# A list scheduler for the second layer of a sigmoid-attention and two-layer kernel, and fixed projection banks in the first layer

## Chip, cores and metric

One core of one Trainium2 chip. The metric is the device time of one execution in microseconds (us); the runs of the kernel before took 1118.6 us in the median of three (1116.41 to 1119.95).

## The reference

Sigmoid attention on 4 batches of 12 heads, sequence 448, head size 64, gives x of 1792 tokens by 768. Two layers follow:

```python
scores = scale * q @ k.T - log(S);  x = (sigmoid(scores) @ v)      # attention, heads side by side
h = x @ w_in                        # 768 -> 2048
x = (h - tanh(h)) @ w_out           # first layer, 2048 -> 768
gate = sigmoid(x @ w_gate)          # 768 -> 1536
x = (gate * (x @ w_val)) @ w_out2   # second layer, 1536 -> 768
```

All inputs of the layers are fp32 values handed over as 64-bit words whose bits the kernel decodes itself.

## The kernel before

**Split numbers.** Each operand of a matmul is split in a high part (ACT copy into fp32r) and a low part (a subtraction on DVE or POOL); a product is three matmuls: high by high, high by low, low by high (`mm3`, L363). A matmul has 128 rows and 448 columns. In tile names, `g`/`gg` are activations (index 0 high, 1 low), `w`, `w_b`, `w_t` weights, `po`/`pq` projections, `ph` hidden sums, `pa pb pc pe` the four PSUM banks of the second layer, `acc` the sums of a layer's output.

**First layer.** 32 steps (N1 = 32): 8 groups of 256 hidden columns, 4 batches each. Step i runs on TensorE the 36 matmuls `ph` of step i+1 (`hidden_mm`) and then the 36 matmuls `po` of step i, six groups of six, one for each 128 output rows (`project_group`, L456). The activation of step i+1 (`hidden_act`, L385) is a chain of ACT instructions (`th sq cut q1 q2`, then the high part) and DVE instructions (`a b c d e`, then the low part `f`). Groups 0, 2 and 4 are added into `acc` by DVE (L471). Groups 1, 3 and 5 are, from step 4 on, seeded: ACT copies the running sum into the bank first (`seed`, L451), the matmuls add to it, and ACT copies it back (L522). All six come out of a pool of four banks, `pb`, in which a new tile takes a bank that was given back; `step` (L501) writes the order of the instructions out by hand, with lists `extra` of things to slip in between groups. LASTSEED = 29 is the first step without seeds.

A weight of the first layer is decoded once (`decode`, L138: one ACT instruction, then four on DVE, L148 to L163). In most first-layer steps one unit of the second layer's weights is decoded as well (`keeping`, tile `mk`) and written to DRAM (`kept`); 21 of 36 units are done so, and the other 15 late, in the second layer, through a tile `mq`, staged in two SBUF buffers.

**Second layer.** 12 blocks (two passes of six; a pass holds two batches). A block has a gate half of seven products (a11, s1, s2, a12, s3, s4, a22: a Strassen-like form over 2 x 2 blocks of activations and weights, `TERMS`, L557), a value half of the same seven, and the twelve projection groups of the block before as fillers between the products of the gate half. A product is nine matmuls, a projection group six. Bank contents move on between products: after a11 ACT copies pa to pb (L720), after s2 pb to pc (L724); s3 adds to pc, and DVE reads the sum (L731 in the gate half, L759 in the value half) before a22 adds to pc again. The value half ends with the high part of `gg` on ACT (L737) and its low part on POOL (L740).

For each block three weight units are loaded from DRAM (`load_m`, L608) and split (`split_pieces`, L616): DVE differences (L639 to L644), ACT highs (L175), POOL lows (L178). When they are issued is decided by `background` (L658): after each product or group it advances a counter by 1.8 or 1.2 us, issues at most one split piece whose load should have come, then loads, then at most one late decode step. `require` (L678) issues whatever a product still needs. The operands of a pass (`operand`, L578) are sums on DVE (L576), highs on ACT (L590) and lows on DVE or POOL (L592); those of pass 0 are placed by hand in steps 29 and 30 and in block 0, those of pass 1 by `turn` (L795) as the value half of block 5 gives places back.

**From the first to the second layer.** The loop at L893 runs steps 0 to 30. After it the first layer's tiles are closed, the PSUM pools are replaced by one with `pa pb pc pe` and four projection banks (L940), the loads and splits are queued, and the projection of step 31 (`groups1`, L484) runs as the fillers of block 0.

Of the kernel before, what the change touches and what calls it, by code (L numbers as in the profile page):

```python
# [32 lines left out]
def kernel(  # L33
# [161 lines left out]

    def keeping(j):
        box = []

        def piece(s):
            def run():  # L200
                if s == 0:
                    if late[0]:
                        if not mq:
                            mq.append(stp.tile([128, 2 * WC], I32, tag="st0", name="mq"))
                        m = mq[0][:, j % 2 * WC:][:, :WC]
                    else:
                        m = wp.tile([128, WC], I32, tag="wh0", name=f"mk{j}")
                    box.append(m)
                    box.extend(decode(NU1 + j, m))
                box[1 + s]()  # L210
                if s == 3:
                    n, h = divmod(j, 2)
                    if h == 0:
                        kept[n] = keep_p.tile([128, 2 * WC], I32, tag=f"kept{n}", name=f"kept{n}")
                    nc.sync.dma_start(out=kept[n][:, h * WC:(h + 1) * WC], in_=box[0])
                    whole.add(j)
# [4 lines left out]
    late = [False]  # L221
    mq = []
# [162 lines left out]
    def hidden_act(i):  # L385
# [45 lines left out]
        def e():  # L431
            nc.vector.copy_predicated(y, mk.bitcast(I32), h)
            nc.scalar.activation(out=gt[:, 0], in_=y, func=AF.Copy)
# [6 lines left out]
        return [sq, th, cut, q1, q2], [a, b, c, d, e, f]  # L440
# [4 lines left out]
    def pb_tile(name):  # L445
        if len(pb_pool) == 1:
            return pb_pool[0].tile([128, 512], F32, tag="pb", name=name)
        n = pb_n[0] = (pb_n[0] + 1) % 4
        return pb_pool[1].tile([128, 512], F32, tag=f"pb{n}", name=name)

    def seed(name, at, d):  # L451
        po = pb_tile(name)
# [3 lines left out]
    def project_group(name, at, gt, outs, d, first, dst=None, po=None, evict=True):  # L456

        seeded = po is not None
        if not seeded:
            po = pb_tile(name)  # L460
# [5 lines left out]
        if not evict:  # L466
            return po
# [16 lines left out]
    def groups1(i):  # L484

        at, gt, outs = outs1(i)
        for d in range(KD):
            def run(d=d):
                project_group(f"po{i}_{d}", at, gt, outs, d, False)
# [4 lines left out]
    LASTSEED = N1 - 3  # L494
# [539 lines left out]
```

## Time and profile before

| | us |
|---|---|
| median of the runs | 1118.6 |
| profiled execution, its own time | 1120.31 |
| span of that execution, first to last instruction | 1118.5 |
| TensorE busy | 1091.0 |
| VectorE (DVE) busy | 816.3 |
| ScalarE (ACT) busy | 613.2 |
| GpSimd (POOL) busy | 407.9 |

Shares are of the span. Matmuls are pipelined, so two that follow each other overlap in the busy time; what TensorE loses is better read from how far apart runs of matmuls start. `x36` after a row is the number of instructions merged in it, and `[0.28 <-ACT acc L522]` says how long the engine was idle before the row and which instruction ended that.

### The profile page before, as it was taken

What the parts mean: (1) busy time and instruction counts of PE and PEld (TensorE: products, weight loads), DVE (VectorE), ACT (ScalarE), POOL (GpSimd) and SP (SyncE); (2) the same over time, 40 slices, a digit from 0 to 9 for tenths busy, and PEclk for the clock granted to TensorE, in tenths of its full rate; (3) what the DMA queues carried; (4) which work ended last, traced back from release to release, by engine and by line L of the source; (5) the groups of instructions that cost most, each with busy time, mean ns of one, the idle gap of its engine ahead of it and who ended that gap; (6) DMA issues with size and microseconds to landing.
All of it is one profiled execution on the core that took longest, in us unless ns stands there. A gap on an engine that the chain in (4) does not pass through costs nothing.

```text
span 1118.5 us, 15946 instructions
## 1 busy us (share of the span) xinstructions
PE 1091.0 (98%) x6085; PEld 967.8 (87%) x6085; DVE 816.3 (73%) x1115; ACT 613.2 (55%) x855; POOL 407.9 (36%) x411
## 2 busy tenths in 40 slices
PE   9999989999999999999999999999998999999998
PEld 5677779998888888899888888988997999999997
DVE  4778657898898989899868979978468555454444
ACT  6778745676767767777656544434336334334320
POOL 5455300011111111011115367566466656446530
PEclk9999999999999999999999999999999999999999
DMA  7666302334242424234300256563111411112102
GB/s 199 189 187 191 115 1 85 99 104 134 81 135 99 142 99 141 87 124 131 112 29 29 98 177 205 166 200 129 57 57 57 156 58 57 58 56 72 70 1 99
DMA packets 40205, 119.79 MB, mean 107 GB/s; under 512 B 6081, under 2 KB 21441, under 8 KB 40129
## 3 DMA queue, kind: packets, MB, share of 16 engines
q1 hardware_dynamic: 36896, 116.38, 32.1%
q0 software_dynamic: 3072, 2.17, 0.9%
q8 instruction: 48, 0.79, 0.3%
q10 hardware_dynamic: 160, 0.23, 0.1%
q14 instruction: 29, 0.23, 0.1%
HBM read 99.09 MB, written 19.66 MB: 106 GB/s over the span
## 4 chain that ended last, share of the span: by engine, by line
PE 87%; DVE 5%; ACT 3%; POOL 2%; issue 1%; DMA 1%; SPq 0%; ACTq 0%; DVEq 0%
PE ph L365 21%; PE po L365 20%; PE pq L365 14%; PE pb L365 6%; PE pa L365 6%; PE pc L365 6%; PE pv L349 5%; PE sa L314 4%; PE pe L365 3%; PE sl L326 1%; POOL a L592 1%; PE pv L342 1%; POOL gg L740 1%; DVE mq L157 0%; DMA st<-in_w_in_dram 0%
## 5 line engine op out<-in xcount | busy, mean ns | idle before, releaser
L365 PE MATMUL po<-g,w 128*128 128x448 f32 x1152 | 246.0, 367 | 3.8 <-DVE acc L471 2.0
L365 PEld LDWEIGHTS po<-g,w 128*128 128x128 f32 x1152 | 210.3, 188 | 33.7 <-ACT acc L522 7.8
L365 PE MATMUL ph<-x,w 128*128 128x448 f32 x1152 | 235.8, 362 | 0.2 <-ACT at L318 0.2
L365 PEld LDWEIGHTS ph<-x,w 128*128 128x128 f32 x1152 | 215.8, 187 | 15.3 <-ACT at L318 0.6
L178 POOL TENSOR_TENSOR w<-m,w 128x384 fp32r<-128x384 f32 x64 | 63.7, 1018 | 389.0 <-ACT w L175 311.8
L365 PE MATMUL pq<-gg,w 128*128 128x448 f32 x864 | 183.8, 363 | 5.0 <-POOL gg L740 2.4
L365 PEld LDWEIGHTS pq<-gg,w 128*128 128x128 f32 x864 | 161.4, 187 | 18.6 <-POOL gg L740 3.1
L178 POOL TENSOR_TENSOR w_t<-mm,w_t 128x384 fp32r<-128x384 f32 x92 | 100.9, 1126 | 129.8 <-ACT w_t L175 54.2
L471 DVE TENSOR_TENSOR acco<-pq,acco 128x448 f32<-128x448 f32 x120 | 72.2, 619 | 33.4 <-PE pq L365 32.9
L365 PE MATMUL pa<-a,w_b 128*128 128x448 f32 x432 | 94.2, 362 | 0.0
L365 PEld LDWEIGHTS pa<-a,w_b 128*128 128x128 f32 x432 | 81.1, 188 | 5.5
L402 ACT ACTIVATE y<-ph 128x896 f32<-128x896 f32 x32 | 29.4, 920 | 78.4 <-PE ph L365 78.4
L471 DVE TENSOR_TENSOR acc<-po,acc 128x448 f32<-128x448 f32 x93 | 57.1, 618 | 20.3 <-PE po L365 20.3
L318 ACT ACTIVATE at<-sa,bias_s 128x896 f32<-128x896 f32 x72 | 67.3, 1008 | 7.9 <-PE sa L314 7.8
L175 ACT ACTIVATE w_b<-mm 128x768 fp32r<-128x768 f32 (+1 forms) x48 | 32.5, 679 | 63.1 <-PE pb L365 30.5
L740 POOL TENSOR_TENSOR gg<-sg,gg 128x448 fp32r<-128x448 f32 x44 | 62.0, 1439 | 13.0 <-ACT gg L737 12.8
L175 ACT ACTIVATE w_t<-mm 128x768 fp32r<-128x768 f32 x48 | 39.9, 842 | 47.9 <-DVE mm L644 34.2
L178 POOL TENSOR_TENSOR w<-mm,w 128x384 fp32r<-128x384 f32 x44 | 48.5, 1124 | 45.5 <-ACT w L175 43.3
L178 POOL TENSOR_TENSOR w_b<-mm,w_b 128x384 fp32r<-128x384 f32 x46 | 51.0, 1130 | 32.7 <-ACT w_b L175 21.7
L349 PE MATMUL pv<-at,vt 128*64 128x224 f32 x576 | 61.3, 363 | 0.0
L145 ACT ACTIVATE m<-st 128x768 f32<-128x768 f32 x32 | 28.9, 903 | 56.7 <-POOL w L178 55.1
L349 PEld LDWEIGHTS pv<-at,vt 128*64 128x64 f32 x576 | 40.1, 140 | 19.7 <-issue 8.0
(102 smaller groups left out, 1861.0 us busy)
## 6 DMA issues: line engine op xcount, KB each, us to landing
mm<-kept SPq DMA_DIRECT2D x36, 768.0 KB, 4.3
st<-in_w_out_dram SPq DMA_DIRECT2D x28, 768.0 KB, 4.5
st<-in_w_in_dram SPq DMA_DIRECT2D x16, 768.0 KB, 4.3
st<-in_w_gate_dram SPq DMA_DIRECT2D x12, 768.0 KB, 5.0
st<-in_w_val_dram SPq DMA_DIRECT2D x12, 768.0 KB, 5.0
kept<-mk SPq DMA_DIRECT2D x21, 384.0 KB, 5.6
kept<-mq SPq DMA_DIRECT2D x15, 384.0 KB, 5.6
kt<-in_k_dram SPq DMA_DIRECT2D x48, 112.0 KB, 4.1
```

Source lines behind the costliest of these rows:

```text
L145: nc.scalar.activation(out=mf, in_=hi.bitcast(F32), func=AF.Abs)
L175: nc.scalar.activation(out=w0, in_=mf, func=AF.Copy)
L178: (low or nc.gpsimd).tensor_tensor(out=w1[:, r], in0=mf[:, r], in1=w0[:, r].bitcast(F32), op=ALU.subtract)
L314: nc.tensor.matmul(pa[:, j, :S], kk[r, ki, c], qq[r, qi], start=(i == 0), stop=(i == 2),)
L318: nc.scalar.activation(out=at[:, :, c], in_=pa[:, :, :S], func=AF.Sigmoid, bias=bias_s, scale=qk_scale,)
L326: nc.tensor.matmul(pl[h * KL:(h + 1) * KL, j, :SH], kt[r, KR:], qt[r, h * SH:(h + 1) * SH], start=True, stop=True,)
L342: nc.tensor.matmul(po[j * D:(j + 1) * D, h, :SH], vt[r, j, NCH - 1], al[r, j], start=True, stop=False,)
L349: nc.tensor.matmul(po[j * D:(j + 1) * D, h, :SH], vt[:, j, c], at[:, j, c, h * SH:(h + 1) * SH], start=False, stop=(c == NCH - 2),)
L365: nc.tensor.matmul(o, w(i), xv(j), start=first and n == 0, stop=last and n == 2, skip_group_check=seeded,)
L402: nc.scalar.activation(out=y, in_=h, func=AF.Tanh)
L471: nc.vector.tensor_tensor(out=at[:, d], in0=po[:, :S], in1=at[:, d], op=ALU.add)
L740: low.tensor_tensor(out=gt[t][:, 1, j], in0=sg[t][:, j], in1=gt[t][:, 0, j].bitcast(F32), op=ALU.subtract,)
```

## The change

1. *First layer, steps 4 to 27.* The four projection banks get fixed places by a table over the parity of the step and the group, and the seed of group 5 is emitted right after the copy-out of group 1, no longer after group 2. In `project_group` all matmuls that read the high part of the activation come first. In product the same: the low operand part is read last.
2. *Steps 28 to 30* run in a new function `tail_step`: step 28 has no seeds (TAIL2 = 28), steps 29 and 30 have seeds of groups 1, 3 and 5, each emitted after the group before it. The activation chain becomes a task.
3. *A list scheduler.* `Task` holds instructions with an engine (v DVE, a ACT, g POOL, s the DMA queue), a planned cost, what they follow and a gate; the tasks are ordered by due time. After each group or product `spend` advances a clock by 1.2 or 1.8 us and issues every task instruction that by the planned costs ends within that slot plus a limit (0.9 us for DVE, 1.0 for ACT; less after some products), or on POOL and the DMA queue starts within it. `must` issues an instruction at once. Weight units, operands, late decodes and the low parts of gg are tasks.
4. *Block 0* has all six groups of step 31 after s2 (SHARE0); its tiles sg and p5 lie in the buffer x7, which before was the second staging buffer of late decodes; that buffer is used for staging again from block 1. The tiles of the first layer are closed, and the second weight unit's buffer opened, when the chain of step 31 has been issued (`settle`).
5. *Block 5* has the fillers in the value half (SHARE_END).
6. Step 27 gets a kept decode, so 22 units are decoded in the first layer and 14 late.

The core of the diff:

```diff
+    SLOT = (
+        {1: 0, 0: 1, 3: 2, 2: 3, 5: 0, 4: 1},
+        {1: 2, 0: 3, 3: 0, 2: 1, 5: 2, 4: 3},
+    )
...
-        for j, (_, w) in enumerate(outs):
-            mm3(
-                po[:, :S], lambda a: w[:, a, d], lambda a: gt[:, a, j],
-                j == 0 and not seeded, j == len(outs) - 1, seeded,
-            )
+        for a, c in ((0, 0), (1, 0), (0, 1)):
+            for j, (_, w) in enumerate(outs):
+                nc.tensor.matmul(
+                    po[:, :S], w[:, a, d], gt[:, c, j],
+                    start=n == 0 and not seeded, stop=n == last, skip_group_check=seeded,
+                )
...
         post(1)
+        pre(5)
         c()
         q2()
         group(2)
-        pre(5)
...
+    def tail_step(i, act, dve):
...
+        def group(d):
+            p = None
+            if d % 2 and i > TAIL2:
+                p = seeds.pop(d)
+            p = project_group(f"po{i}_{d}", at, gt, outs, d, False, p, evict=False)
+            if d % 2 == 0 and i > TAIL2:
+                seeds[d + 1] = must("a", 0.55, lambda: None) and seed(f"po{i}_{d + 1}", at, d + 1)
+            spend(1.2)
...
+        chain = Task(f"c{i}", now[0] + (9.0 if i < N1 - 2 else 3.0))
...
+        def start(self):
+            kinds, f, after, gate = self.ops[self.at]
+            t = 0.0 if gate is None else gate()
+            if t is None:
+                return None
+            t = max([t, now[0]] + [self.end[i] for i in after])
+            ways = [(max(t, busy[e]) + cost, max(t, busy[e]), e) for e, cost in kinds.items()]
+            if len(ways) > 1 and not self.haste and ways[1][0] < self.due - SPARE:
+                return ways[1]
+            return min(ways)
...
+    def spend(length, ease=0.9, ease_a=1.0):
+        if last_chain and last_chain[0].at == len(last_chain[0].ops):
+            settle()
+        end = now[0] + length
...
+                if (t if e in "gs" else done) > end + (dict(v=ease, a=ease_a).get(e, 0.0)):
+                    continue
+                task.go(at)
...
+            kinds = dict(v=0.6, g=1.3) if FLEX or n in (0, 1, 2, 18) else dict(g=1.3)
+            task.add(kinds, low(slice(0, HC), False), [h])
+            return task.add(kinds, low(slice(HC, None), True), [h])
...
+            t = task.add(dict(v=1.2), ta, [b1, b22])
+            t = task.add(dict(v=0.7), lambda: tb(0), [t])
+            t = task.add(dict(v=0.7), lambda: tb(1), [t])
...
+        t = task.add(dict(a=0.95), a, (), gate)
+        t = task.add(dict(v=1.4), lambda: box[2](), [t])
+        t = task.add(dict(v=1.2), lambda: box[3](), [t])
+        task.add(dict(v=1.2), c2, [t])
...
+            spend(1.8, 0.2 if term == "s3" else 0.9, 0.4 if term in ("a11", "s2") else 0.8)
...
+        def finish(t, ready):
+            task = g_task[k, t] = Task(f"g{k}_{t}", now[0] + (6.0 if t == 0 else 8.0))
...
+                task.add(dict(v=0.7, g=1.4) if FLEX or k == NK - 1 else dict(g=1.4), f, [h])
...
+    SHARE0 = dict(s2=12)
+    SHARE = dict(s2=2, a12=4, s3=7, s4=10, a22=12)
+    SHARE_END = dict(a11=2, s1=4, s2=6, a12=8, s3=10, s4=12)
```

SPARE is 2.0 us, FLEX and SEED are False.

## Rows read from the trace of the kernel before

**Rows 1.** The page, busy time of the engines over the span.
```profile
PE 1091.0 (98%) x6085; PEld 967.8 (87%) x6085; DVE 816.3 (73%) x1115; ACT 613.2 (55%) x855; POOL 407.9 (36%) x411
```

**Rows 2.** The chain of waits, in order of time: start us, us.
```profile
217.68 7.56 PE po L365 x36
...
557.31 7.57 PE po L365 x36
564.87 7.21 PE ph L365 x36
...
655.91 2.40 PE pq L365 x12
...
906.09 2.40 PE pq L365 x12
...
1064.49 2.40 PE pq L365 x12
```

**Rows 3.** Waits from 214 to 565 us: total us, times, longest us.
```profile
PEld po L365 <- ACT acc L522: 6.8, 24, 0.3
PEld po L365 <- ACT po L453: 6.3, 24, 0.3
```

**Rows 4.** Timeline of one step, 453 to 461 us (start us, us).
```profile
453.59 4.80 PEld L365 LDWEIGHTS po<-g,w 128*128 128x128 f32 x24
...
458.10 0.52 ACT L522 ACTIVATE acc<-po 128x448 f32<-128x448 f32 x1
...
458.67 1.11 PEld L365 LDWEIGHTS po<-g,w 128*128 128x128 f32 x6 [0.28 <-ACT acc L522]
...
459.45 0.53 ACT L453 ACTIVATE po<-acc 128x448 f32<-128x448 f32 x1
...
460.04 1.11 PEld L365 LDWEIGHTS po<-g,w 128*128 128x128 f32 x6 [0.26 <-ACT po L453]
```

**Rows 5.** Timeline of TensorE from step 30 into block 0.
```profile
610.01 1.48 PE L365 MATMUL po<-g,w 128*128 128x448 f32 x6 [2.04 <-DVE acc L471]
...
619.56 1.28 PE L365 MATMUL po<-g,w 128*128 128x448 f32 x5 [1.14 <-DVE g L436]
...
646.90 3.59 PE L365 MATMUL pc<-a,w_t 128*128 128x448 f32 x9 [2.07 <-DVE pe L759]
```

**Rows 6.** Waits of TensorE over the span; then its timeline near the end.
```profile
PE pc L365 <- DVE pe L759: 4.9, 3, 2.1
PE pb L365 <- ACT pb L720: 3.2, 4, 1.1
...
PE pq L365 <- POOL gg L740: 2.4, 2, 1.8
...
1099.25 0.47 PE L365 MATMUL pq<-gg,w 128*128 128x448 f32 x1 [0.56 <-ACT gg L737]
1099.91 14.48 PE L365 MATMUL pq<-gg,w 128*128 128x448 f32 x71 [0.19 <-DVE gg L740]
```

**Rows 7.** Windows: length, busy us (count) of PE PEld DVE ACT POOL, clock, DMA.
```profile
480.00:510.00 30.00, 30.00 (x148) 26.99 (x147) 28.06 (x35) 21.70 (x32) 3.99 (x4) 1.00 0.40 132
648.00:651.00 3.00, 3.00 (x12) 2.67 (x11) 2.97 (x5) 0.83 (x1) 0.12 (x1) 0.64 0.58 205
690.00:730.00 40.00, 39.79 (x198) 36.63 (x197) 35.75 (x45) 18.33 (x28) 26.33 (x22) 1.00 0.57 186
890.00:930.00 40.00, 40.00 (x202) 37.49 (x201) 19.30 (x28) 14.94 (x23) 21.78 (x21) 1.00 0.18 62
```

**Rows 8.** Single lines: count, shortest, median, longest ns, first and last start us.
```profile
L157 DVE SCALAR_TENSOR_TENSOR mk<-st,mk x21: 957/959/960, 171.8 to 543.0; 128x768 int32<-128x768 int32 x21
L157 DVE SCALAR_TENSOR_TENSOR mq<-st,mq x15: 952/1515/1914, 635.5 to 772.9; 128x768 int32<-128x768 int32 x15
L639 DVE TENSOR_TENSOR mm<-mm x24: 944/950/1917, 580.8 to 1062.3; 128x768 f32<-128x768 f32 x24
L740 POOL TENSOR_TENSOR gg<-sg,gg x44: 1132/1470/1877, 651.2 to 1063.3; 128x448 fp32r<-128x448 f32 x44
```

More of the change, by code (lines that the diff above doesn't have):

```diff
@@ L194, with parked @@
     early = []
+    def parked(j, m):
+        n, h = divmod(j, 2)
+        if n not in kept:
+            kept[n] = keep_p.tile([128, 2 * WC], I32, tag=f"kept{n}", name=f"kept{n}")
+        nc.sync.dma_start(out=kept[n][:, h * WC:(h + 1) * WC], in_=m)
+        whole.add(j)
     def keeping(j):
@@ L211, in run @@
                 if s == 3:
[L212 to L216, printed above, removed]
+                    parked(j, box[0])
             return run
         return [piece(s) for s in range(4)]
-    late = [False]
-    mq = []
     whole = set()
@@ new lines, in prepare, with known, gate, one @@
+        done_at = {}
+        def known(*names):
+            def gate():
+                got = [done_at.get(n, free(n[4:]) if n[:4] == "free" else None) for n in names]
+                return None if None in got else max(got)
+            return gate
+        BEFORE = dict(
+            s1=("freesums1",), s2=("freesums2", "sums1", "a11"), s4=("freesums4", "sums2", "s1"),
+            s3=("freesums3", "sums4", "s2"),
+        )
+        def one(term, due):
+            task = op_task[ps, term] = Task(f"x{term}_{ps}", due)
+            after = []
+            task.haste = term in BEFORE
+            if term in BEFORE:
+                def add(c):
+                    def f(eng):
+                        sums(term, ps, c, eng)
+                        task.haste = c < KH - 1
+                        if c == KH - 1:
+                            done_at["sum" + term] = task.end[-1]
+                    return f
+                for c in range(KH):
+                    after = [task.add(dict(v=0.7, g=1.4), add(c), (), known(*BEFORE[term]))]
+            def high():
+                xo[ps, term] = x_tile(PLACE[ps][term], f"{term}_{ps}")
+                nc.scalar.activation(out=xo[ps, term][:, 0], in_=src[term], func=AF.Copy)
+            h = task.add(dict(a=1.35), high, after, known("free" + term))
+            for c in range(KH):
+                def low(eng, c=c):
+                    t = xo[ps, term]
+                    eng.tensor_tensor(
+                        out=t[:, 1, c], in0=src[term][:, c], in1=t[:, 0, c].bitcast(F32),
+                        op=ALU.subtract,
+                    )
+                    if c == KH - 1:
+                        done_at[term] = max(task.end)
+                task.add(dict(v=0.7, g=1.4), low, [h])
@@ L596 @@
+        for i, term in enumerate(TERMS):
+            one(term, due + 1.8 * i)
     m_t = {}
     wk = {}
-    done = {"slot": 0}
-    FETCH = 6.5
-    loads = []
-    splits = []
     order = [0, 1]
@@ L688, with require_x @@
+    BASE = dict(s2=("s1", "a11"), s4=("s2", "s1"), s3=("s4", "s2"))
+    def require_x(ps, term):
+        if ps:
+            for j in sorted(de_task):
+                de_task[j].finish()
+        for other in BASE.get(term, ()):
+            require_x(ps, other)
+        op_task[ps, term].finish()
     PRODUCT = {
@@ L946 @@
-        pb_pool.append(pm[0])
-        late[0] = True
-        late_u.append(NU1 + NPRE - len(early) // 4)
-        fetch(late_u[0] + 1)
-        preps += [
-            lambda: operand(0, "s3", nc.vector), lambda: operand(0, "s4", nc.vector),
-            lambda: operand(0, "a22", nc.vector),
-        ]
-        free_at[0] = 16.0
-        for n in order[1:]:
-            loads.append(n)
-            splits += split_pieces(n)
+            if i >= TAIL2:
+                chain = tail_step(i, act, dve)
+                for term in {TAIL2: ("a11", "a12"), TAIL2 + 1: LATER}.get(i, ()):
+                    x_free[0, term] = now[0] + 0.5
+                continue
```

564 lines of the change are left out of this document (383 added, 181 removed).

## The prediction

> **What bounds the kernel now.** I read the page's engine line first: TensorE is counted busy for 98% of the span [rows 1]. Overlapping matmuls count as busy, so this says only that TensorE is the bound; what it loses has to be read from the pace. The chain of waits gives the pace: 12 matmuls of 448 columns take 2.40 us and a ph run of 36 takes 7.21, 0.200 us each [rows 2]. From step 4 to step 27 each po run of 36 takes 7.56 or 7.57 us instead. The excess over 0.200 us per matmul, stage by stage, all from [rows 2]:
>
> - Steps 4 to 27: from 217.68 to 557.31 lie 23 steps, 339.63 us against 23 x 14.40 = 331.20, and the 24th loses 0.37 more: **8.8 us**.
> - Transition, 564.87 to 655.91: ph of steps 29 to 31 (108 matmuls), po of 28 to 31 (144), block 0 (126) and three products of block 1 (27) are 405 matmuls, 81.0 us; it takes 91.04: **10.0 us**.
> - Blocks 1 to 6, 655.91 to 906.09: six blocks of 198 matmuls are 237.6 us; it takes 250.18: **12.6 us**.
> - Blocks 7 to 11: 906.09 to 1064.49 is 158.40, exactly 4 x 39.6: **nothing**.
> - The end: TensorE idles 0.56 us, and the next matmuls start 0.66 instead of 0.20 us later [rows 6]: **1.0 us**.
>
> Together 32.4 us. No order of this work can save more than that after 217 us, as nothing of the arithmetic goes.
>
> The waits name what ends the loss. In the steps it is ACT twice, 24 times each [rows 3]. In one step [rows 4] group 4's weight load starts at 458.67, right after ACT's copy-out at 458.10 (L522, the eviction of group 1), so group 4 sits in group 1's bank; group 5's load starts at 460.04, after the seed of group 5 at 459.45 (L453), which ACT runs behind q2. In the transition TensorE waits 2.04 us for a DVE sum, 1.14 us for the low half of g31, then 2.07 us for a DVE read of pc [rows 5]. After that last wait nine matmuls take 3.59 us, where nine take 1.8; the clock granted in 648 to 651 is 0.64 of full, so part of that stretch ran at 1.2 GHz [rows 7]. In the second layer the waits are for a DVE read of pc or pe (4.9 us), for ACT's copy into pb (3.2 us), and for POOL's low halves gg (2.4 us) [rows 6]. DVE is loaded where they lie: 35.75 of 40 us in 690 to 730, where late decodes run, 19.30 in 890 to 930, where none do [rows 7].
>
> **Part by part.** *Fixed banks and an earlier seed (steps 4 to 27).* With the table, group 4 takes group 0's bank, evicted by DVE long before, and group 5 takes group 1's. The seed of group 5 is emitted straight after the copy-out of group 1 and ahead of q2. In the step shown ACT ends that copy at 458.62; the seed takes 0.53 and ends near 459.15. The loads of groups 0 to 3 begin at 453.59 [rows 4], so group 5's is due five groups of 1.2 us later, at 459.59. So both waits go. q2 comes 0.5 us later; behind it on ACT stand the copy of a weight and the copy-out of group 3, and DVE's L427 waits for it, by up to 0.5 us; DVE's idle time covers that in a step without a kept decode. In steps with a kept decode DVE is busy 28.06 of 30 us [rows 7], 13.8 us of a 14.77 us step, under the new 14.40. If that cover were gone the step would stay at 14.77. Bounds 0 to 8.8 lost; I take 0.3 left, since the margin on the seed is 0.4 us.
>
> *High halves first.* Same number of matmuls and loads; a low half is now read 0.8 us into a projection group and 1.2 us into a product. It costs nothing, and takes up to 0.8 us off waits like the 1.14 us on g31 and the 0.19 us at the end.
>
> *Steps 28 to 31 and block 0.* Step 28 loses its seeds: six DVE sums instead of three, 1.9 us more on DVE, in a step with no decode. The kept decodes become 22 and the late ones 14; one decode moves from DVE's loaded stretch into step 27, with its fetch and its write to DRAM on SP's queue, long before block 3 reads it. Steps 29 and 30 get three seeds each. Such a seed is put on ACT right after the group before it, behind whatever background work the scheduler has already issued there, up to 1.0 us past the end of the slot by its own costs. A group lasts 1.2 us, so each of the six can be late by 0 to 0.9 us (1.0, a copy-out and a seed of 0.55, less 1.2): 0 to 5.4, and I take 1.0, as ACT's real costs (0.53 for a copy against 0.55 planned) run ahead of the plan. The activation chain of step 31 no longer stands behind operand work by position: it has the earliest due time. Its twelve instructions of about 1 us need some 10 us, and 7.2 + 3 x 1.8 = 12.6 us pass between ph31 and po31. I take 1.0 (0 to 3.2, the first two waits of [rows 5]). The second weight unit is loaded only when that chain has ended, 3 to 6 us into block 0; by the planned costs load 5.0, first split 2.1, differences 2.6 and second split 2.1 make 11.8, and the value half starts 19.8 us into the block: 1.5, bounds 0 to 5. Together **3.5 left of 10.0**, with bounds 0 to 13.6, so a loss is possible here.
>
> *Blocks 1 to 6.* Background work on DVE may run at most 0.2 us past the product s3, and on ACT 0.4 us past a11 and s2. The DVE join then ends 0.85 us after s3, and a22, which overwrites what it reads, comes 1.8 us after it; the pb and pc copies have the same 1.8 us. These are the waits of [rows 6]. The late decodes get one staging buffer in block 0 instead of two, and their due times spread them further: 14 decodes of about 3 us on DVE. In block 5 the projections of block 4 go into the value half, so the operands of pass 1 get 27 instead of 12.6 us to replace those of pass 0. Behind each join on DVE stand only sums into four rotating banks, 3.6 us of slack. I take **2.0 left of 12.6**; bounds 0 to 12.6.
>
> *What speaks against it* is the two-input work on DVE. A decode's L157 takes 957 to 960 ns in the first layer, where POOL is nearly idle, and 1515 ns in the median, 1914 at most, in block 0 to 3 [rows 8]; L639 goes from 950 to 1917. The planner costs these at 1.2 always. The extra 0.97 us of an L639 ahead of a join puts its end at 1.82 us, still at the edge, so by the rows I add nothing to the 2.0. The Trainium skill (SBUF — State Buffer, Who interferes with whom) says that a DVE instruction with two SBUF inputs and a POOL instruction that reads SBUF exclude each other, the second waiting for the whole of the first; the doubled rows agree. By that rule a join behind one 1877 ns POOL instruction [rows 8] would end at 2.7 us and cost 0.9; on all 12 gate and value joins of six blocks that is 11, and the time about 1104.
>
> *The end*: 0.8 of 1.0 left, since the joins and the high half still follow s4. Blocks 7 to 11 have nothing to win.
>
> **Sum.** Left are 0.3 + 3.5 + 2.0 + 0.8 = 6.6 of 32.4, a gain of 25.8. The profiled execution took 1120.3 (span 1118.5 and 1.8 around it), so 1094.5; the median of the runs, 1118.6, stands 1.7 under it: **1092.8, say 1093**.
>
> **Rivals.**
> 1. *DVE stays late where POOL works.* The planner advances its clock by 1.8 and 1.2 us whatever happens and knows no interference, so DVE runs behind its plan in the transition and in the blocks with decodes. For: the stretched rows [rows 8] and 35.75 of 40 us [rows 7]. Against: decodes are spread, and lows of operands and first weights can go to either engine. The transition keeps its 10.0 and blocks 1 to 6 half of 12.6: gain 8.5 + 6.3 + 0.2 = 15.0, **1104**. (The Trainium skill's rule, in SBUF — State Buffer, would bring it about; by its count above the time is the same.)
> 2. *The first layer keeps its pace*, because DVE at 13.8 of 14.4 us takes over as soon as ACT's two waits go. For: 0.6 us a step is little room. Against: each fourth step to step 20 has no kept decode and lets DVE catch up. The 8.5 go: **1101**.
> 3. *The order barely changes*: the scheduler puts second-layer work about where the hand-written counters put it, and the change is its banks alone. For: blocks 7 to 11 were at 39.6 by hand. Against: the s3 and a11 limits target waits that are there. Gain 9.5: **1109**.
> 4. *Slower: POOL's low halves gg come late.* In most blocks the lows of weights and of gg may run on POOL alone. gg of half 0 is read 1.8 + 5.4 + 0.8 = 8.0 us after s4 ends; two joins and the high half by plan (2.3) and two lows at 1470 ns [rows 8] need 5.2, so 2.8 us of margin. If the scheduler issues five or more weight lows ahead, 1.0 to 1.5 us each, all 36 matmuls of a half stand behind the wait in TensorE's queue. At 3.0 us in 11 blocks that is 33: **1126**; from 2.3 us a block on, the gain is gone. Against: POOL is busy 21.78 of 40 us [rows 7], gg has a due time 6 or 8 us ahead, and POOL work is issued only when it can start within the slot; today it cost 2.4 us in all.
>
> **How the numbers follow.** Forecast 0.62, rivals 1 to 4: 0.17, 0.10, 0.06, 0.05. A measurement here tells 0.3%, 3.4 us, from no change. All but rival 4 are faster by more; part of a bad transition together with rival 3 could land within it: 0.02. The forecast's own range is 1088 (1.5 us left) to 1099. Rivals 1 and 2 are taken in, 3 and 4 left out: 1087 to 1105.
>
> **What would show it.** Right: po runs of 7.20 in steps 4 to 27, no ACT releaser there; ph29 to the first pq in under 86 us; no wait for pe L759 or pb; blocks 1 to 6 at 39.6 to 40.2; no stretch with a lower clock in block 0. Wrong: 7.5 us po runs (rival 2); pc waiting for DVE behind an instruction of 1.5 us or more (rival 1); equal stalls at the same products (rival 3); pq waiting for POOL in block after block (rival 4).

## The result and the profile after

The changed kernel took 1104.97 us in the median of four runs (1104.83 to 1105.82), the kernel before 1117.71 beside it (1116.41 to 1119.95): a ratio of 0.9882, with the 95% interval from 0.9866 to 0.9897. A second set of runs gave 1103.62 against 1118.48, 0.9876 (0.9859 to 0.9892). So it is faster by 1.2%, some 13 us, about half of the 25.8 forecast, and the time lies inside the range only just, at its upper edge of 1105.

The profiled execution took 1104.88, with a span of 1103.1: 15.4 us under the 1118.5 of before. The profiled execution of before (1120.31) was 2.6 us slower than the median of the runs beside after, so stages read from the two profiles add up to more than the 13 us of the medians. The losses below are worked out as in the prediction, as what TensorE's matmuls start later than 0.200 us after one another.

| stage | before | forecast left | after |
|---|---|---|---|
| steps 4 to 27 | 8.8 | 0.3 | 0.3 |
| transition, ph of step 29 to the first pq | 10.0 | 3.5 | 7.8 |
| blocks 1 to 6 | 12.6 | 2.0 | 8.6 |
| blocks 7 to 11 | 0 | 0 | 0 |
| end | 1.3 | 0.8 | 1.7 |
| sum | 32.7 | 6.6 | 18.4 |

On TensorE's timeline of after ph of step 29 starts at 555.47, the first pq at 644.24 and that of block 7 at 890.44, so the transition takes 88.77 against 81.0 and blocks 1 to 6 take 246.2 against 237.6. The end of before is 1.3 by the same measure, not the 1.0 of the prediction: the first pq starts 0.73 us late, not 0.56, and the next 0.46, with 0.11 behind it. The sums differ by 14.3; another 0.8 us had gone before step 4 (the first row of the chain below stands at 216.91, that of [rows 2] at 217.68), which differs by more than that between executions of one kernel (po of step 4 starts at 216.75 in this profile of after and at 215.41 in a second one), and the last 0.3 lies behind the last matmul.

The page of after, its busy time (as [rows 1]) and the granted clock in 40 slices of the span:

```profile
PE 1084.3 (98%) x6085; PEld 974.2 (88%) x6085; DVE 809.3 (73%) x1112; ACT 617.7 (56%) x861; POOL 427.4 (39%) x432
...
PEclk9999999999999999999999899999999999999999
```

The busy shares tell as little as before. The one 8 in the clock's line is the slice from 607 to 634 us, which comes back below.

The chain of waits of after, in order of time (start us, us), as [rows 2]:

```profile
216.91 7.21 PE po L468 x36
...
548.42 7.21 PE po L468 x36
555.63 7.20 PE ph L361 x36
...
890.60 2.40 PE pq L468 x12
...
1049.00 2.40 PE pq L468 x12
```

The po runs of 7.56 are now 7.21. From 890.60 to 1049.00 lie 158.40 us, four blocks at 39.6, as before.

The waits of after from 214 to 565 us (total, times, longest), as [rows 3]:

```profile
...
ACT y L398 <- PE ph L361: 40.3, 24, 3.2
DVE acc L481 <- PE po L468: 11.5, 6, 3.7
...
```

ACT and DVE wait for TensorE, as they did before. No row of PE or PEld is left in this view; both ACT releasers of [rows 3] are gone. The timeline of one step shows why (as [rows 4]):

```profile
447.16 7.20 PEld L468 LDWEIGHTS po<-g,w 128*128 128x128 f32 x36
...
451.67 0.52 ACT L536 ACTIVATE acc<-po 128x448 f32<-128x448 f32 x1
...
452.22 0.55 ACT L456 ACTIVATE po<-acc 128x448 f32<-128x448 f32 x1
...
452.70 1.03 ACT L407 ACTIVATE s<-mk,gb 128x896 f32<-128x896 f32 x1
```

All 36 loads are one unbroken row. The seed of group 5 ends at 452.77; the load of that group is due at 447.16 + 5 x 1.2 = 453.16. The margin is the 0.4 us that the prediction had worked out.

**Where the rest stayed.** The waits of TensorE in after, over the span (total, times, longest), as the first part of [rows 6]:

```profile
PE pq L468 <- POOL gg L1064: 3.5, 3, 1.8
...
PE pb L999 <- ACT pb L1012: 1.8, 1, 1.8
PE po L468 <- ACT g L431: 1.6, 1, 1.6
...
PE pq L468 <- DVE w L853: 1.1, 1, 1.1
PE pb L999 <- DVE s L768: 0.8, 1, 0.8
```

The wait for the DVE read of pc or pe is gone, and of four pb waits one is left. What is left lies in two places. The first is block 0. The timeline of after there (start us, us; in brackets the idle time and what ended it):

```profile
594.82 0.55 ACT L585 ACTIVATE acc<-po 128x448 f32<-128x448 f32 x1 [1.81 <-PE po L468]
...
595.73 0.91 ACT L395 ACTIVATE u<-ph 128x896 f32<-128x896 f32 x1
...
602.01 1.10 DVE L423 SCALAR_TENSOR_TENSOR ph<-s,ph 128x896 f32<-128x896 f32 x1
...
603.81 2.65 DVE L768 TENSOR_TENSOR s<-acc,s 128x448 fp32r<-128x448 f32 x3 [0.70 <-ACT s L762]
...
606.38 1.17 DVE L428 COPY_PREDICATED y<-mk,ph 128x896 f32<-128x896 int32 x1
606.51 0.47 PE L999 MATMUL pb<-s,w_t 128*128 128x448 f32 x1 [0.80 <-DVE s L768]
...
608.58 10.61 PE L468 MATMUL po<-g,w 128*128 128x448 f32 x36 [1.60 <-ACT g L431]
...
610.58 8.24 PEld L468 LDWEIGHTS po<-g,w 128*128 128x128 f32 x32 [0.76 <-DVE g L434]
```

The activation chain of step 31 begins at 592.10 (y, L398) and its high half ends just before 608.58. Its second ACT instruction stands in ACT's queue behind a copy-out (594.82) for which TensorE had not yet finished the group, so ACT does nothing for 1.81 us; and its last DVE instruction before the high half (606.38) stands behind three low parts of an operand, some 3.3 us after the chain's DVE instruction before it (602.01) ended. TensorE waits 0.80, does one matmul, waits 1.60, and then needs 10.61 us for 36 matmuls that take 7.36 elsewhere.

The second place is the boundary between the passes, the end of block 5 and the start of block 6:

```profile
841.42 1.33 ACT L762 ACTIVATE s<-acc 128x1344 fp32r<-128x1344 f32 x1 [0.23 <-DVE acc L629]
...
842.65 0.83 ACT L842 ACTIVATE w<-mm 128x768 fp32r<-128x768 f32 x1
842.82 1.63 POOL L768 TENSOR_TENSOR s<-acc,s 128x448 fp32r<-128x448 f32 x1 [1.98 <-ACT s L762]
842.85 4.79 DVE L768 TENSOR_TENSOR s<-acc,s 128x448 fp32r<-128x448 f32 x4
843.38 0.53 ACT L1012 ACTIVATE pb<-pa 128x448 f32<-128x448 f32 x1
...
843.96 2.08 PE L999 MATMUL pb<-s,w_t 128*128 128x448 f32 x9 [1.78 <-ACT pb L1012]
...
847.12 5.94 POOL L1064 TENSOR_TENSOR gg<-sg,gg 128x448 fp32r<-128x448 f32 x4
...
848.68 0.47 PE L468 MATMUL pq<-gg,w 128*128 128x448 f32 x1 [1.85 <-POOL gg L1064]
...
850.15 2.88 PE L468 MATMUL pq<-gg,w 128*128 128x448 f32 x7 [0.99 <-POOL gg L1064]
```

ACT's copy into pb stands behind the high part of an operand, which itself waited for a DVE sum, and behind the high part of a weight. Then the low halves of gg on POOL come late.

Windows of after (length, busy us and count of PE PEld DVE ACT POOL, clock, DMA), and below them one of before, as [rows 7]. Block 6 starts 19.1 us later in before than in after, and so does this window, to hold the like work as 797 to 850 of after:

```profile
609.00:615.00 6.00, 5.86 (x16) 4.71 (x16) 5.33 (x6) 3.59 (x4) 3.82 (x4) 0.52 0.40 131
690.00:730.00 40.00, 40.00 (x201) 37.49 (x201) 36.26 (x47) 17.51 (x28) 28.35 (x21) 1.00 0.59 195
797.00:850.00 53.00, 48.53 (x239) 44.30 (x238) 43.86 (x51) 27.20 (x36) 43.92 (x35) 1.00 0.17 56
848.00:853.00 5.00, 3.33 (x9) 2.74 (x10) 4.59 (x4) 0.00 (x0) 5.00 (x4) 0.73 0.46 157
```

```profile
816.10:869.10 53.00, 48.13 (x235) 43.42 (x234) 40.68 (x47) 25.57 (x34) 35.85 (x27) 1.00 0.13 46
```

In 609 to 615 the granted clock is 0.52, so TensorE ran at 1.2 GHz nearly throughout. The 36 matmuls took 10.61 - 7.36 = 3.25 us more than elsewhere. Not all of that is the clock: the restart and the wait of a weight load for the low half of g31 (0.76 us on PEld) are in it. In experiment 5 the same 36 took 7.80 us behind a like wait at full clock, so the clock cost some 2.8 us. In 690 to 730, where the late decodes run, DVE is fuller than before (36.26 against 35.75 us) and TensorE loses nothing. Towards the boundary POOL is busy 43.92 of 53 us where it had 35.85 at the like place, and DVE 43.86 where it had 40.68.

**At the end** the planner gave two of the last four low halves of gg to POOL. The timeline of after:

```profile
1083.77 1.07 PE L468 MATMUL pq<-gg,w 128*128 128x448 f32 x4 [0.56 <-ACT gg L1059]
1083.86 3.04 POOL L1064 TENSOR_TENSOR gg<-sg,gg 128x448 fp32r<-128x448 f32 x2 [12.27 <-ACT gg L1059]
...
1085.45 13.88 PE L468 MATMUL pq<-gg,w 128*128 128x448 f32 x68 [0.61 <-POOL gg L1064]
```

POOL needs 3.04 us for two; TensorE waits 0.61 us, where in [rows 6] it waited 0.19 for DVE.

### The profile page after: what moved, and what is told of

Its sections match the earlier page's. It is cut to its first block, busy times and chain, and to the rows that moved or that the text cites. A ratio compares the mean times of both kernels' runs of the same rounds, so it can differ in the third digit from the quotient of the medians.

```text
span 1103.1 us, 15973 instructions
## 1 busy us (share of the span) xinstructions
PE 1084.3 (98%) x6085; PEld 974.2 (88%) x6085; DVE 809.3 (73%) x1112; ACT 617.7 (56%) x861; POOL 427.4 (39%) x432
## 4 chain that ended last, share of the span: by engine, by line
PE 93%; DVE 3%; ACT 2%; POOL 1%; issue 1%; DMA 0%; SPq 0%; ACTq 0%; POOLq 0%
PE ph L361 21%; PE po L468 21%; PE pq L468 15%; PE pa L999 8%; PE pc L999 7%; PE pb L999 7%; PE pv L345 5%; PE sa L310 4%; PE pe L999 3%; PE sl L322 1%; PE pv L338 1%; DMA st<-in_w_in_dram 0%; PE pz L1173 0%; ACT at L314 0%; POOL gg L1064 0%
## 5 line engine op out<-in xcount | busy, mean ns | idle before, releaser
L468 PE MATMUL po<-g,w 128*128 128x448 f32 x1152 | 240.0, 366 | 2.1 <-ACT g L431 1.6
L468 PEld LDWEIGHTS po<-g,w 128*128 128x128 f32 x1152 | 216.0, 189 | 21.0 <-ACT g L431 1.9
L468 PE MATMUL pq<-gg,w 128*128 128x448 f32 x864 | 184.4, 364 | 5.1 <-POOL gg L1064 3.5
L468 PEld LDWEIGHTS pq<-gg,w 128*128 128x128 f32 x864 | 162.5, 188 | 17.8 <-POOL gg L1064 4.5
L853 POOL TENSOR_TENSOR w_t<-mm,w_t 128x384 fp32r<-128x384 f32 x90 | 96.8, 1105 | 137.9 <-ACT w_t L842 137.5
L853 POOL TENSOR_TENSOR w_b<-mm,w_b 128x384 fp32r<-128x384 f32 x54 | 59.8, 1128 | 15.0 <-ACT w_b L842 13.3
L1064 POOL TENSOR_TENSOR gg<-sg,gg 128x448 fp32r<-128x448 f32 x42 | 55.1, 1341 | 24.4 <-ACT gg L1059 24.4
L398 ACT ACTIVATE y<-ph 128x896 f32<-128x896 f32 x32 | 29.4, 919 | 59.2 <-PE ph L361 59.0
L853 POOL TENSOR_TENSOR w<-mm,w 128x384 fp32r<-128x384 f32 x44 | 47.1, 1094 | 21.3 <-ACT w L842 20.7
L310 PE MATMUL sa<-sp 64*128 64x448 f32 x432 | 51.1, 376 | 0.2 <-ACT at L314 0.2
```

The lines of the kernel that those rows point to most:

```text
L310: nc.tensor.matmul(pa[:, j, :S], kk[r, ki, c], qq[r, qi], start=(i == 0), stop=(i == 2),)
L398: nc.scalar.activation(out=y, in_=h, func=AF.Tanh)
L468: nc.tensor.matmul(po[:, :S], w[:, a, d], gt[:, c, j], start=n == 0 and not seeded, stop=n == last, skip_group_check=seeded,)
L853: eng.tensor_tensor(out=w1[:, r], in0=quarters(lo, hi)[:, r], in1=w0[:, r].bitcast(F32), op=ALU.subtract,)
L1064: eng.tensor_tensor(out=gt[t][:, 1, j], in0=sg[t][:, j], in1=gt[t][:, 0, j].bitcast(F32), op=ALU.subtract,)
```

## The experiments

Eleven further kernels ran, and the kernel after once more. Edits are against the kernel after, except in the first and in the hand-ordered one. A kernel with one execution is named so. A loss is the sum of TensorE's excess over 0.200 us per matmul in the stage.

**1. The banks and the seed alone**, put into the kernel before:

```diff
+    SLOT = (
+        {1: 0, 0: 1, 3: 2, 2: 3, 5: 0, 4: 1},
+        {1: 2, 0: 3, 3: 0, 2: 1, 5: 2, 4: 3},
+    )
...
+        pre(5)
         c()
         q2()
         group(2)
-        pre(5)
```

> The kernel before with the table of banks and the earlier seed of group 5 alone; no scheduler. Theory: these two edits carry the whole first-layer gain, po runs of 7.2 us in steps 4 to 27, and the second layer stays as it was: 8.8 us off, about 1109. Rival (DVE takes over as the pace of the steps): po runs stay above 7.4 us, under 4 us off, about 1114.

It took 1109.65 against 1119.9: 0.9914 (0.9896 to 0.9931), some 9.6 us less. The po runs are 7.21, steps 4 to 27 lose 0.3, the transition 10.7, blocks 1 to 6 12.4, the end 1.3. So this part alone carries most of the gain, and the whole scheduler adds only what lies between 0.9914 and 0.9882, 3.6 us, whose intervals just overlap; between the two profiled spans (1109.5 and 1103.1) it is 6.4, but there the profiled execution (1111.27) was the slowest of its four, 1.6 above their median.

**2 and 3. Which of the two it is.** First the table with the banks of groups 4 and 5 changed back, so that group 4 again follows ACT's copy-out of group 1; then the seed of group 5 back behind group 2:

```diff
-        {1: 0, 0: 1, 3: 2, 2: 3, 5: 0, 4: 1},
-        {1: 2, 0: 3, 3: 0, 2: 1, 5: 2, 4: 3},
+        {1: 0, 0: 1, 3: 2, 2: 3, 5: 1, 4: 0},
+        {1: 2, 0: 3, 3: 0, 2: 1, 5: 3, 4: 2},
```

> The changed kernel with group 4 in group 1's bank and group 5 in group 0's, as before, and the early seed kept. Theory: group 4 waits again for ACT's copy-out of group 1, 0.18 us a step, 24 steps: 4.4 us more, about 1109, with ACT L585-like copy-outs as releaser. Rival (the early seed alone removed both waits): 1105, po runs of 7.2.

```diff
-        pre(5)
         c()
         q2()
         group(2)
+        pre(5)
```

> The changed kernel with the seed of group 5 back behind q2 and group 2, the new banks kept. Theory: group 5 waits for its seed again, 0.16 to 0.19 us a step: 4 to 4.5 us more, about 1109. Rival (the banks alone removed both waits): 1105.

One execution each: 1109.57 and 1112.95. The waits from 214 to 565 us that name TensorE's load, first with the old banks, then with the late seed:

```profile
PEld po L468 <- ACT acc L536: 6.7, 24, 0.3
```

```profile
PEld po L468 <- ACT po L456: 10.8, 24, 0.5
```

With the old banks the po runs take 7.40 and steps 4 to 27 lose 4.8, as expected. With the late seed they take 7.57 and the steps lose 8.9, all of what before lost and twice what I had expected. The two waits overlap: group 4 starting 0.3 us earlier only makes TensorE wait longer for the same seed (0.5 instead of 0.3). The table by itself gives nothing, the earlier seed by itself 4.0, both together 8.5.

**4. A filler of block 0 later.** The po groups of step 31 stand after a12, one product (1.8 us) later:

```diff
-    SHARE0 = dict(s2=12)
+    SHARE0 = dict(a12=12)
```

> The changed kernel with the projections of step 31 one product later in block 0 (after a12 instead of after s2). Theory: the chain of step 31 ends 1.6 us too late for po31, and the half-speed matmuls after it follow from TensorE's idle time there; 1.8 us of other work in between removes the wait and the slow stretch, 4 to 6 us off, about 1100, clock 1.00 between 600 and 620. Rival (the chain is pushed back by the operand work that products force ahead of it, so the wait moves along): 1104 to 1106, still a wait on ACT's high half before po31.

1103.44 (1101.58 to 1103.95), 0.9851 (0.983 to 0.9872). The transition loses 4.5 instead of 7.8: the 1.60 us wait has shrunk to 1.05 (now for g's low half), and from 604 to 614 the clock is 1.00. But block 1's wait for the second weight unit (w L853) grew from 1.1 to 2.9 us, and after it some matmuls ran at the lower clock again (0.83 in 641 to 651, 1.7 us of excess). Blocks 1 to 6 lose 12.0 instead of 8.6, so that all losses come to 18.6 in this profile against 18.4 in after: what the transition gained was lost again behind it, and the interval of the ratio overlaps that of after.

**5. No seeds in step 30; gg of block 5 on DVE or POOL; the last gg on DVE alone:**

```diff
-            if d % 2 and i > TAIL2:
+            if d % 2 and i == TAIL2 + 1:
...
-                task.add(dict(v=0.7, g=1.4) if FLEX or k == NK - 1 else dict(g=1.4), f, [h])
+                task.add(
+                    dict(v=0.7, g=99.0) if k == NK - 1 else dict(v=0.7, g=1.4) if k == NBLK - 1
+                    else dict(g=1.4), f, [h]
+                )
```

> The changed kernel with three edits in separate stages: step 30 without seeds (its six sums on DVE), the low halves gg of block 5 on DVE or POOL as the planner likes, those of the last block on DVE alone. Theory (ACT idles up to 1.8 us behind copy-outs that wait for TensorE, and the chain of step 31 stands behind them): without seeds in step 30 the chain ends 2 to 3 us earlier, the 1.6 us wait on g31 and the slow stretch after it go, 5 us off in the transition. Rival (the chain is late because products force s2's operand ahead of it on DVE): under 1 us off there. Boundary: the waits on gg (1.85 + 0.99 us) fall under 1 us if POOL's queue is the cause, the wait for pb (1.8 us) stays. End: 0.7 us off.

One execution, 1101.70. The transition loses 2.5. TensorE's timeline there, and the window that was slow in after:

```profile
606.63 7.80 PE L468 MATMUL po<-g,w 128*128 128x448 f32 x36 [1.51 <-ACT g L431]
```

```profile
609.00:615.00 6.00, 6.00 (x32) 5.62 (x31) 6.00 (x10) 2.59 (x3) 4.02 (x4) 1.00 0.31 124
```

The step 30 seeds themselves had cost TensorE only 0.9 us, but with them gone the chain's ACT part no longer stands behind copies that wait for groups, and the chain takes 14.0 us instead of 16.4. The wait on g31 did not go, as the theory had it: TensorE comes earlier too, and a single wait of 1.51 us is left, but the clock stays at 1.00 behind it. Of the 5.2 us gained, 2.8 are the clock, 1.3 the waits for the operand s, 0.9 the seeds and 0.2 the wait on g31. The run does not say which engine had held the chain up, since POOL now makes the first lows of s, which no longer stand ahead of the chain on DVE either. At the boundary the edit made it worse: a row of the waits reads `PE pq L468 <- DVE gg L1064: 5.3, 1, 5.3`, the stage loses 10.8 instead of 8.6. The planner put these low halves on DVE, where they came later still than on POOL. The end loses 1.07.

**6. The operands of pass 0 due earlier**, and the lows of the weight unit of the boundary on POOL alone:

```diff
-            kinds = dict(v=0.6, g=1.3) if FLEX or n in (0, 1, 2, 18) else dict(g=1.3)
+            kinds = dict(v=0.6, g=1.3) if FLEX or n in (0, 1, 2) else dict(g=1.3)
...
-            prepare(0, T0 - 4.0, lambda term: x_free.get((0, term)))
+            prepare(0, T0 - 10.0, lambda term: x_free.get((0, term)))
```

> The changed kernel with the operands of pass 0 due 6 us earlier, and the low halves of weight unit 18 on POOL alone. Transition, theory (s2's operand is planned behind the chain and then forced in front of its instruction e): with it due before the chain the waits on s2 (0.8 us) and on g31 (1.6 us) and the slow stretch go, 5 to 7 us off. Rival (ACT has too much to do in step 30 whatever the order): the wait on g31 stays at 1 us or grows. Boundary: if DVE is late there because it takes unit 18's lows, the wait for pb (1.8 us) falls under 0.5; if POOL is the one that is late, the waits on gg grow over 3 us.

One execution, 1107.98. The wait for s is gone, and `PE po L468 <- ACT g L431: 4.9, 1, 4.9` stands in its place: transition 9.4. Due times push the delay from one reader to the next; they make no room. The loss of blocks 1 to 6 is about the same (8.9): the pb wait went to 0.8, the one for gg grew to 2.3.

**7. The low halves of gg on DVE alone** in blocks 0, 5 and 11:

```diff
-                task.add(dict(v=0.7, g=1.4) if FLEX or k == NK - 1 else dict(g=1.4), f, [h])
+                task.add(
+                    dict(v=0.7, g=99.0) if k in (0, NBLK - 1, NK - 1) else dict(g=1.4), f, [h]
+                )
```

> The changed kernel with the low halves gg of blocks 0 and 5 (and 11) on DVE alone. In block 1 DVE now takes 5.34 us for four lows of weight unit 2 (0.54 us each when alone) beside POOL's four gg lows of 1.43 us. Theory (the two engines hold each other off): with gg's lows on DVE too, each low of unit 2 takes 0.55 us, DVE does all eight in about 4.7 us, less than the four took before, and the 1.1 us wait for w does not grow. Rival (DVE simply has too much): the four lows still take over 1 us each, or all eight take 7 us or more, and TensorE waits 3 us. Boundary: waits on gg under 1 us, and the wait for pb as before or longer, since DVE has 2.5 us more to do.

One execution, 1105.36. In block 1 gg and the weight's lows now follow each other on DVE. The timeline there:

```profile
640.14 2.41 DVE L1064 TENSOR_TENSOR gg<-room,gg 128x448 fp32r<-128x448 f32 x2
...
640.95 2.48 POOL L853 TENSOR_TENSOR w_t<-mm,w_t 128x384 fp32r<-128x384 f32 x2 [0.24 <-issue]
...
642.71 1.60 DVE L853 TENSOR_TENSOR w<-mm,w 128x384 fp32r<-128x384 f32 x2 [0.16 <-ACT w L842]
644.23 1.15 DVE L1064 TENSOR_TENSOR gg<-room,gg 128x448 fp32r<-128x448 f32 x2
645.30 1.01 DVE L853 TENSOR_TENSOR w<-mm,w 128x384 fp32r<-128x384 f32 x2
```

While POOL works (to 643.43) two pieces of gg take 2.41 us; after it the like two take 1.15, and two of w 1.01. In after the same weight pieces ran beside POOL's gg and took 1491 ns in the median:

```profile
L853 DVE TENSOR_TENSOR w<-mm,w x4: 1082/1491/1511, 642.1 to 646.0; 128x384 fp32r<-128x384 f32 x4
...
L157 DVE SCALAR_TENSOR_TENSOR mq<-st,mq x14: 941/1195/1800, 628.6 to 779.5; 128x768 int32<-128x768 int32 x14
```

The late decodes (L157) are stretched less than before: 1195 ns in the median, where [rows 8] had 1515 and where the decodes of the first layer take 957. All eight pieces took 6.17 us on one engine; I had expected 4.7, having forgotten that other POOL work would run beside the first two. The wait for w fell from 1.1 to 0.3. At the boundary the expectation of under 1 us failed: TensorE waited 5.3 us for DVE's gg, the stage lost 9.1.

**8. Fillers later in blocks 0, 1 and 6, the last gg on DVE alone:**

```diff
+    SHARE0 = dict(a12=12)
+    SHARE1 = dict(s3=6, s4=9, a22=12)
+    SHARE6 = dict(a12=4, s3=7, s4=10, a22=12)
...
-        share = SHARE0 if k == 0 else SHARE
+        share = {0: SHARE0, 1: SHARE1, NBLK: SHARE6}.get(k, SHARE)
```

> The changed kernel with fillers later where they wait: po31 after a12 in block 0, pq of block 0 after s3 in block 1, pq of block 5 after a12 in block 6; the last low halves gg on DVE alone. Theory (nothing is short of throughput; single results come 1 to 3 us after TensorE wants them, and each idle time of some 2 us costs a slow stretch on top): transition 4 us off, the wait for w of block 0's projection gone, boundary 3 us off with the wait for pb still there, end 0.7 off: 8 us, about 1097. Rival (the engines are behind, so the waits reappear at the next products): 1102 or more.

1096.17 (1096.0 to 1097.07), 0.9801 (0.9784 to 0.9819). The transition loses 4.5, blocks 1 to 6 lose 3.7, the end 1.1. Block 1's wait for w is gone with no stretch at a lower clock from 641 to 651 (1.00), and `PE pq L468 <- POOL gg L1064` is down to 1.9 in two waits. The pb wait of 1.8 us went too, though no line of the edit moves that copy: the tasks fall into other slots.

**9. Both together**, step 30 without seeds and fillers later, those of blocks 1 and 6 only from s3 on, and none at s2 in any block:

```diff
-            if d % 2 and i > TAIL2:
+            if d % 2 and i == TAIL2 + 1:
...
+    SHARE0 = dict(a12=12)
+    SHARE1 = dict(s3=6, s4=9, a22=12)
+    SHARE = dict(a12=4, s3=7, s4=10, a22=12)
...
+        share = {0: SHARE0, 1: SHARE1, NBLK: SHARE1}.get(k, SHARE)
```

> The changed kernel with step 30 unseeded, po31 after a12, the fillers of all blocks from a12 on (in blocks 1 and 6 from s3 on) and the last gg lows on DVE. Theory (each remaining wait is one late result, and its place is free to move): of the 9 us still lost after step 27 when the fillers were moved, s2's waits (1.8 us) and the wait for g31 (1.3 us) go, the waits on gg at blocks 2 and 6 (1.2 and 1.4) fall under 0.5 each: 4 to 6 us under that kernel, about 1091, no slow stretch. Rival (moving fillers later delays what stands behind them, such as the sums of the pass boundary or the weights' places): 1096 or more, with new waits at products.

1097.9 (1096.06 to 1098.78), 0.9818 (0.9803 to 0.9832): no better. The transition loses 1.5, but blocks 1 to 6 lose 8.3. TensorE in block 6:

```profile
843.30 0.47 PE L999 MATMUL pc<-s,w_t 128*128 128x448 f32 x1 [1.87 <-DVE s L768]
844.78 1.11 PE L999 MATMUL pc<-s,w_t 128*128 128x448 f32 x2 [1.00 <-DVE s L768]
```

With the fillers gone from between a12 and s3, s3 comes earlier than its operand. Two waits, one matmul between them, and then a stretch at the lower clock (0.72 from 841 to 853).

**10. The later fillers without the scheduler**, in the kernel of experiment 1:

```diff
-        share = dict(s2=2, a12=4, s3=7, s4=10, a22=12)
+        share = dict(a12=4, s3=7, s4=10, a22=12)
```

> The kernel before with fixed banks and early seed (no scheduler) and its fillers from a12 on in every block. Theory (the scheduler is what removes the waits for pb and pc in blocks 1 to 5; late fillers help only what waits for gg and g31): 2 to 4 us under the banks-only kernel, about 1106, waits for pb and for DVE's read of pc still 5 us or more. Rival (the places of the fillers were the whole matter, not the list scheduler): 1098 or less.

One execution, 1108.82 against 1118.48, the same 0.9914 as experiment 1; its losses are 1.1 us smaller. Its waits for DVE's read of pe are 5.6 us in all and for pb 2.4. With the order by hand this move of the fillers buys almost nothing.

**11. Block 6's fillers back from a12 on**, else as 9:

```diff
-        share = {0: SHARE0, 1: SHARE1, NBLK: SHARE1}.get(k, SHARE)
+        share = {0: SHARE0, 1: SHARE1}.get(k, SHARE)
```

> The combined kernel with block 6's fillers from a12 on instead of from s3 on. Theory (with the fillers after s3 block 6 comes to s3 7.2 us earlier than the low half of its s3 operand, which DVE makes between POOL's instructions; from a12 on 4 groups of fillers cover it): the waits on DVE L768 in block 6 and the slow stretch after them, 6.3 us, become about 1.5 us of waits on gg: 4 to 5 us under the combined kernel, ratio about 0.978, 1093 by a before of 1118.5. Rival (the boundary is short of DVE time, so the wait reappears as one on gg or on another operand): 1097 or more.

1093.45 (1091.99 to 1094.08), 0.9773 (0.9759 to 0.9787), span 1091.7: faster than both kernels, 1.1% under after. The transition loses 1.7, blocks 1 to 6 3.9, the end 1.1. Its windows, the first of them 5.6 us earlier than in after, as its block 6 is:

```profile
791.40:844.40 53.00, 51.30 (x253) 46.81 (x252) 44.33 (x50) 28.49 (x38) 50.35 (x40) 1.00 0.22 75
840.00:846.00 6.00, 4.70 (x22) 3.82 (x21) 6.00 (x5) 0.96 (x2) 6.00 (x5) 1.00 0.04 12
```

POOL is busier towards the boundary than in after (50.35 against 43.92 of 53) and DVE about as busy (44.33 against 43.86), and the loss is less than half. The expectation's figure for how much earlier s3 had come was a slip: four groups are 4.8 us, not 7.2.

**12. The kernel after once more**, beside 9 and 10; its times stand with the result:

> The changed kernel itself, on the chip of the two that follow. All theories: 0.988 of the time before, some 1105 to 1107 by this chip.

Its profile loses 7.9 us in the transition, 8.6 in blocks 1 to 6 and 1.7 at the end, at the same places.

## Why the prediction was right or wrong

The first layer came out as worked out; the rest did not, and that the time lies in the range is luck. The sum gave 6.6 us left and 18.4 were measured, and the range reached up to 1105 only because rivals 1 and 2 were taken in, and neither says where the time was lost. Of the signs named for being right, the pace of steps 4 to 27 and the end of the waits for pe came; the transition under 86 us (88.77), no wait for pb (one of 1.8) and no lower clock in block 0 (0.52 in 609 to 615) did not.

**Steps 4 to 27: right.** 0.3 left was forecast and 0.3 measured, with the margin as worked out, and the cover on DVE held at 28.77 of 30 us in 480 to 510. Rival 2 (this stage keeps its pace) fell. What I did not see is that the waits of [rows 3] lie behind each other: counted as 6.8 and 6.3 they look like two halves, while the table alone is worth nothing (experiment 3).

**Transition: mis-sized, 3.5 against 7.8.** The terms, with what TensorE's starts show in after:
- Seeds of steps 29 and 30: 1.0 forecast; their groups lost 0.9 in step 30 and at most 0.4 in step 29. Right at their own place. But they held up ACT, and the chain of step 31 with it: taking those of step 30 away took 5.2 off the stage (experiment 5; its other edits act later). That is close to the 5.4 of the upper bound, by another road, since more than half of it is the lower clock, which went with them.
- The wait on g31: "I take 1.0" is the step that failed. The chain has the earliest due time, as I said, but a due time counts only when an instruction is issued. Once a copy-out that waits for TensorE is in ACT's queue (1.81 us idle), or an operand's lows in DVE's (some 3.3 us), the chain stands behind it. From 592.10 to 608.58 it took 16.5 us, not the some 10 of its durations, against 12.6 of cover. Waits 0.80 and 1.60, with the restarts 2.95 us of excess.
- The stretch at 1.2 GHz: some 2.8 us of the 3.25 that the 36 matmuls lost. I had the like in [rows 7], and gave it no price in what would be left. With the waits shorter, or one of them gone, the clock does not fall (experiments 4 and 5).
- Second weight unit: 1.5 forecast; it shows as 1.29 us of excess in front of block 1's pq, counted with blocks 1 to 6.

**Blocks 1 to 6: mis-sized, 2.0 against 8.6.** The limits on s3 and a11 did what was forecast: no wait for a read of pc or pe, and blocks 1 to 5 lose little but that 1.29. What failed is "the operands of pass 1 get 27 instead of 12.6 us", from which I concluded that the boundary was free. They get the time, but share it with gg, the sums and a weight unit on two engines that hold each other up, and in queues that keep their order. The boundary lost 1.95 (pb copy), 3.3 (two waits for gg) and 1.7 us at the lower clock (0.73 in 848 to 853). Moving two groups from s2 to a12, 1.8 us of room for gg, took most of that away (experiments 8 and 11).

**The rivals.** The time is the one I had put on rival 1, DVE late where POOL works. But the place is another. Rival 1 wanted half of blocks 1 to 6 lost at the joins, where the late decodes run; 690 to 730 is fuller on DVE than before and loses nothing. The mechanism is there, as experiment 7 shows in rows (gg pieces of 1.2 us beside POOL, 0.6 without), and stretched rows stand where operands have a date, in block 0 and at the boundary; how much of the loss there is theirs is not shown. The Trainium skill (SBUF — State Buffer, Who interferes with whom) states that a DVE instruction with two SBUF inputs contends with a POOL instruction that reads SBUF. The rows of experiment 7 agree. The prediction's count by the Trainium skill's rule, 0.9 us on each gate and value join, did not come: no wait for a join's read of pc or pe is left. Rival 3 was wrong about the order, since its joins' waits did go; but by size the banks were indeed the greater half (experiment 1). Rival 4's mechanism, POOL's gg late, occurs at two places, the boundary and the end, not in eleven blocks, and costs the 3.5 us of its row before the clock.

**The end: mis-sized.** 0.8 forecast, 1.7 measured, where before lost 1.3: I took it that the low halves would stay on DVE as in [rows 6]; the planner's choice of POOL is in the diff I read. With DVE alone it is 1.1.

Not settled: how the remaining excess divides between the two engines' holding each other up and the order of the queues. No run took one away and kept the other. That POOL is busier in experiment 11 than in after and DVE no less, with less lost, speaks for the order, or for where the dates lie, as the larger share, but does not show it. Nor did a run take the order of the halves (the low part read last) by itself; experiment 1 shows only that the first layer's gain does not need it.

## What to carry to other kernels

A due time orders what is issued, not what is already in an in-order queue: a chain with a date is held up by whatever was put ahead of it that itself waits for something, so ask of each filler what it waits for, and give the reader of a late tile more distance (move the fillers of TensorE) before moving due times. Two waits that stand close behind each other in every step can be one delay with two releasers: their sum is no guide to what removing one gives. Give a stretch at the lower clock a price in every forecast that leaves waits of a microsecond or two close together; here one cost 1.7 to 2.8 us.

## What the runs showed that was not expected

In block 0 of after, TensorE idled 0.80 us, did one matmul, idled 1.60 us, and then started its matmuls 0.37 us apart (16 in 609 to 615, granted clock 0.52). The lower clock cost some 2.8 us, more than both waits together. In experiment 5 one wait of 1.51 us stood there and in experiment 4 waits of 0.80 and 1.05 with fourteen matmuls between them; behind both the clock stayed at 1.00. At the other place the waits of 2.91 us (experiment 4, block 1) and 5.30 (experiment 5, boundary) were again followed by matmuls at the lower clock, 1.7 and 2.7 us of excess. So in block 0 the two waits cost more than twice what they lasted. Two waits with one matmul between them were followed by the lower clock at the boundary of after (1.85 and 0.99) and in experiment 9 (1.87 and 1.00) as well. The length of a single wait does not sort the cases: in before one of 2.07 us was followed by slow matmuls (nine in 3.59 us), while one of 2.04 (both in [rows 5]) and one of 2.13, in front of the nine matmuls at 855.64 that took 2.08 us, were not. What decides it, no run here shows.

That two-input instructions on DVE stretch beside POOL was in [rows 8], and so was a wide spread of POOL's own gg pieces (1132 to 1877 ns). After shows where these stretch: in block 1, beside DVE's weight pieces, a gg piece took 1463 ns in the median, over the other blocks 1160.

```profile
L1064 POOL TENSOR_TENSOR gg<-sg,gg x42: 1150/1160/1876, 682.3 to 1085.4; 128x448 fp32r<-128x448 f32 x42
L1064 POOL TENSOR_TENSOR gg<-room,gg x4: 1456/1463/1475, 642.8 to 647.0; 128x448 fp32r<-128x448 f32 x4
```
